# Sigmoid attention and a mixer in one kernel: which unit does which share of the channel products

## The chip, the cores and the metric

The kernel runs on one core of one Trainium2 chip. The metric is the device time of one execution in microseconds; the time before is 366.64 us, the median of three runs (366.64 to 368.11).

## The reference

Eight batches of twelve attention heads, 448 positions of 64 features, with a sigmoid in place of a softmax. The result, as 448 x 768 per batch, goes through a mixer: a token product over the positions (448 to 256 to 448) with a residual, then a channel product over the features (768 to 1536 to 768) with a residual.

```python
scores = scale * np.matmul(q, k.transpose(0, 1, 3, 2)) - np.log(S)
attn = 1.0 / (1.0 + np.exp(-scores))
x = np.matmul(attn, v)                        # as (8, 448, 768)
xt = x.transpose(0, 2, 1)
h = np.maximum(xt @ w_tok1, 0.0) @ w_tok2     # token product
u = x + h.transpose(0, 2, 1)
h2 = np.maximum(u @ w_ch1, 0.0) @ w_ch2       # channel product
out = u + h2
```

## The kernel before

The instructions stand in the order in which the code issues them (`tc.manual_schedule()`); each engine works through its own list in order and waits on semaphores that the tile framework places. All products take 16-bit floats and accumulate in PSUM.

**Units.** The twelve heads of a batch are worked on four at a time, so a batch has NU = 3 units u = 0, 1, 2, and there are 24 of them; unit c is batch c // 3, u = c % 3. In unit c TensorE does:

- `qk`, seven score steps (j = 0 to 6). Each is four products on 64x64 quarters of the array (L174) into one of two score tiles; ScalarE then makes one sigmoid of it (L181).
- `av` for unit c - 1: the value product, 28 quarter products (L201) into two PSUM banks, cast by VectorE to xT (L210). `xtrans_dma` (L225), on SP's queue, transposes xT into xn.
- the token product of unit c - 2: `tok_tail` (L260, quarter tiles) and `tok1` (L279, full tiles), two relus on ScalarE (L293), then `ytrans` (L300), the second token product, whose result VectorE adds to xT, giving u (L307).
- a share of the channel products of an earlier batch: `ch1` (twelve tiles of 128 channels, six products each, L333; relu on VectorE, L345) and `ch2` (for three blocks t of 128 positions two halves of 384 features, twelve products each, L402; the addition of u on VectorE, L426), and `ch2_last`, the half block of 64 positions that remains (24 products of 128x64, two side by side, L486; L511). Batch 0's u has no transposed copy `un`, so there TensorE adds it, by products with the identity (L414, L497).

**Quarter products of the channel part.** `ch1_pair` and `ch2_pair` do a part of two such tiles with the 64x64 quarters of the array (`quads`, L357), four at once, so that the array keeps the shape that the scores and the value product have. `turn0` and `turn1` are the two passes over the rows of the array; `ch2_pair` does eight of the twelve terms so and leaves four for each half to `rest` (L462), on full tiles.

**PSUM.** The two score tiles take four of the eight banks; the other four, m0 to m3, are handed out by `bank`, in turn from `at_bank`. A tile that gets a bank waits for the reader of the tile that had it. `keep_open` skips a bank in which a tile is being accumulated.

**Stages.** An opening written out by hand does units 0 to 3 and the first two tiles of batch 0's ch1. A first loop (L728 on, `range(N_FIRST, ONE_RUN)`) does units 4 to 8, with the channel work cut into pieces (`pieces_ch1`, `pieces_ch2`, `pieces_last`) and set between groups of score steps by shares: batch 0's remaining ch1 and its ch2 over units 4 to 7, batch 1's ch1 in unit 8. A second loop does units 9 to 23, where all work on quarter tiles is in one run: score steps 0 and 1, `turn0`, step 2, `av` with step 3, step 4, `turn1` with step 5, `tok_tail`, step 6. Behind the run come, on full tiles, `rest`, `tok1`, pieces of channel work and `ytrans`. Of batch b - 2, u = 0 does the c2 pair of t = 0 and the half block, u = 1 the c2 pair of t = 1 and both halves of t = 2 in full tiles; of batch b - 1, u = 2 does a c1 pair and the other ten tiles of ch1. A closing does the last value and token products, batch 6's ch2 and batch 7's channel products.

**Loads.** q, k, v and the weights come by POOL's queue (`load`). From batch 2 on q and k are put into another order by VectorE (`relayout`, L119, three for each) and transposed by a DMA on SP's queue (`dma_transpose`, L132), in the list `through_dma`, of which the loops take one item at a time (`copies.pop(0)()`). `gated_loads(b)` on POOL waits, by a small copy (L714), for the transposed q of batch b + 1, and then issues the loads of v for batch b + 1 and of k and q for batch b + 2. `utrans` transposes u into `un` on SP's queue.

Of the kernel before, what the change touches and what calls it, by code (L numbers as in the profile page):

```python
# [22 lines left out]
NU = 3  # L23


@with_exitstack
def kernel(
# [46 lines left out]
    at_bank, open_bank = [0], [None]  # L74
# [9 lines left out]
    def keep_open(is_open):  # L84
        open_bank[0] = (at_bank[0] + 3) % 4 if is_open else None
# [239 lines left out]
    def ch1(b, cb, d0=0, d1=NDB):  # L325
        if cb == 0 and d0 == 0:
            h2[b] = pa.tile([128, NCB, S], FP16, tag="h2", bufs=1, name=f"h2_{b}")
        if d0 == 0:
            acc[b, cb] = bank([128, 512], FP32, f"c1_{b}_{cb}")
            keep_open(b != 0 or cb > 1)  # L330
        ps = acc[b, cb]
        for d in range(d0, d1):
            nc.tensor.matmul(  # L333
                out=ps[:, 0:S],
                lhsT=c1[:, BY_UNIT[d], 128 * cb : 128 * cb + 128],
                rhs=uts[b % 2][:, BY_UNIT[d], 0:S],
                start=(d == 0),
                stop=(d == NDB - 1),
            )
        if d1 == NDB:  # L340
            keep_open(False)
            ch1_out(b, cb, ps)
# [22 lines left out]
    def ch1_pair(b, cb):  # L365

        if cb == 0:
            h2[b] = pa.tile([128, NCB, S], FP16, tag="h2", bufs=1, name=f"h2_{b}")
        ps = [bank([128, 512], FP32, f"c1_{b}_{cb + p}") for p in range(2)]

        def step(turn, d):
            quads(
                ps,
                S,
                turn,
                lambda p, part, m: c1[
                    part, BY_UNIT[d], 128 * (cb + p) + m : 128 * (cb + p) + m + 64
                ],
                lambda p, part: uts[b % 2][part, BY_UNIT[d], 0:S],
                d == 0,  # L380
                d == NDB - 1,
            )
            if turn == 1 and d == NDB - 1:
                for p in range(2):
                    ch1_out(b, cb + p, ps[p])

        turns = [[lambda t=t, d=d: step(t, d) for d in range(NDB)] for t in range(2)]
        return turns[0], turns[1], lambda: None

# [3 lines left out]
    def ch2(b, t, half, n0=0, n1=NCB):  # L393
        cols = slice(DH * half, DH * half + DH)
        if n0 == 0:
# [3 lines left out]
            keep_open(True)  # L399
# [11 lines left out]
        keep_open(False)  # L411
        if b not in un:
            for n in range(NU):
                nc.tensor.matmul(  # L414
                    out=ps[:, 128 * n : 128 * n + 128],
                    lhsT=uts[b % 2][:, NU * half + n, 128 * t : 128 * t + 128],
                    rhs=ident[:, :],
                    start=False,
                    stop=(n == NU - 1),
                )  # L420
        ch2_out(b, t, half, ps)

# [18 lines left out]
    def ch2_pair(b, t):  # L441
# [17 lines left out]
        def rest():  # L459
            for p in range(2):  # L460
                for n in range(n_quads, NCB):
# [5 lines left out]
                        stop=(n == NCB - 1),  # L467
                    )
                ch2_out(b, t, p, ps[p])
# [256 lines left out]
    ONE_RUN = 3 * NU  # L726
    pending, copies = [], []
    for c in range(N_FIRST, ONE_RUN):  # L728
        b, u = divmod(c, NU)
        before = divmod(c - 1, NU)  # L730


        if c in (N_FIRST, 2 * NU + 2):
# [26 lines left out]
        if c == 2 * NU + 2:  # L760
            copies += through_dma(3, 0)[NU + 1 :]
# [14 lines left out]
        if c == 2 * NU + 1:  # L776
            copies = through_dma(3, 0)[: NU + 1]
        spent += work(2)
        if c == 2 * NU + 2:
            utrans(b - 1)  # L780
# [8 lines left out]
        if c + 1 == ONE_RUN:  # L789
            at_bank[0] = 0  # L790
# [9 lines left out]
    for c in range(ONE_RUN, N_CYCLES):  # L800
# [20 lines left out]
        qk(b, u, 2)  # L821
        if u == 2:
            utrans(b - 1)
        av(*before, 0, 4)
# [9 lines left out]
        at_bank[0] = 0  # L834
# [11 lines left out]
        at_bank[0] = 0  # L846
# [23 lines left out]
    for f in work[20:]:  # L870
# [33 lines left out]
```

## Time and profile before

| | |
|---|---|
| runs | 366.64, 368.11, 366.64 us |
| profiled execution | 366.46 us, of which the profile's span is 364.7 |
| granted TensorE clock | 0.999 |
| TensorE's products by line, busy us | ch1 L333 100.6; qk L174 60.3; ch2 L402 58.1; av L201 41.0; quarter products L357 32.0 (c2) and 14.9 (c1) |
| sigmoids L181 | 168 of 1015 ns, 155.6 us busy |

A row of the timeline has the start in us, the length, engine, line, operation, output <- inputs, their sizes and the count of instructions merged into it; in square brackets stands the idle time of the engine just before, with what ended it. Products overlap: the next one starts before the one before has ended, so what a product costs is read from start to start and not from its length. A row of the stages has the stretch, its length, and for each engine the busy time and the count of instructions, then the clock, the DMA engines' share and GB/s. "PEld" is TensorE's loading of weights.

### The profile page before, as it was taken

The page shows a single profiled execution, that of the slowest core. Times are in us where ns is not written, and L with a number is a line of the kernel's source. Part 1 is how long each engine was busy: PE and PEld are TensorE (multiplying, and loading weights), DVE is VectorE, ACT ScalarE, POOL GpSimd, SP SyncE. Part 2 cuts the span into 40 slices and gives each one's busy share as a digit, 9 for nine tenths or more (in the row PEclk, how much of TensorE's full clock was granted, in tenths as well). Part 3 has the DMA queues.
Part 4 walks back from the last instruction along what each step waited for, and adds up shares of the span by engine and source line. Part 5 has one row for each costly group of instructions (what it writes and reads, how often), then busy time and mean ns, then how long its engine had stood idle before and what let it go on. Part 6 is the DMA issues. An engine that isn't in the chain of part 4 may idle for free.

```text
span 364.7 us, 8938 instructions
## 1 busy us (share of the span) xinstructions
PE 354.8 (97%) x3968; PEld 207.2 (57%) x3968; DVE 186.2 (51%) x343; ACT 171.3 (47%) x214; POOL 52.8 (14%) x91
## 2 busy tenths in 40 slices
PE   8889999999999999999999999999999999999995
PEld 5555455556556665665655665566656665555563
DVE  3466547355645456455554565455553445525531
ACT  2996545767246770664516761664607751010000
POOL 8875500120120002200040001300010000000000
PEclk9999999999999999999999999999999999999999
DMA  8999999999999398977989497987983274137014
GB/s 146 163 192 203 204 204 193 141 182 213 181 174 162 80 165 157 191 132 154 182 132 215 70 190 149 176 149 147 174 134 81 59 155 43 31 86 130 23 45 108
DMA packets 103958, 52.09 MB, mean 143 GB/s; under 512 B 76016, under 2 KB 100848, under 8 KB 103920
## 3 DMA queue, kind: packets, MB, share of 16 engines
q1 hardware_dynamic: 78880, 29.70, 43.8%
q0 software_dynamic: 24816, 21.50, 38.2%
q8 instruction: 31, 0.51, 0.5%
q10 hardware_dynamic: 224, 0.33, 0.3%
q14 instruction: 7, 0.06, 0.1%
HBM read 43.45 MB, written 11.01 MB: 149 GB/s over the span
## 4 chain that ended last, share of the span: by engine, by line
PE 89%; DMA 4%; POOL 4%; ACT 1%; DVE 0%; issue 0%; POOLq 0%
PE c L333 27%; PE c L402 15%; PE c L357 11%; PE qk L174 9%; PE xa L201 8%; PE yt L300 5%; PE tk L279 5%; PE c L486 5%; PE c L462 4%; DMA raw_q<-in_q_dram 2%; DMA raw_v<-in_v_dram 2%; POOL raw_q L108 1%; POOL raw_k L108 1%; POOL raw_v L108 1%; ACT att L181 1%
## 5 line engine op out<-in xcount | busy, mean ns | idle before, releaser
L181 ACT ACTIVATE att<-qk,att_bias 128x896 f16<-128x896 f32 x168 | 155.6, 1015 | 119.7 <-PE qk L174 119.0
L333 PE MATMUL c<-ut,c 128*128 128x448 f16 x516 | 100.6, 353 | 0.7 <-DVE h L345 0.7
L345 DVE TENSOR_SCALAR h<-c 128x448 f16<-128x448 f32 x96 | 59.2, 623 | 46.9 <-PE c L333 46.0
L333 PEld LDWEIGHTS <-c 128*128 128x128 f16 x516 | 49.6, 98 | 48.4 <-issue 4.4
L174 PE MATMUL qk<-tr_q,tr_k 64*64 64x448 f16 x672 | 60.3, 357 | 2.1 <-ACT att L181 2.0
L402 PE MATMUL c<-c,h 128*128 128x384 f16 x336 | 58.1, 326 | 0.0
L210 DVE CAST xT<-xa 128x448 f16<-128x448 f32 x48 | 27.7, 619 | 40.2 <-PE xa L201 40.2
L426 DVE TENSOR_TENSOR o<-un,c 128x384 f32<-128x384 f16 x42 | 23.3, 554 | 46.1 <-PE c L402 31.0
L402 PEld LDWEIGHTS <-h 128*128 128x128 f16 x336 | 32.1, 98 | 21.7 <-issue 1.8
L201 PE MATMUL xa<-att,raw_v 64*64 64x448 f16 x672 | 41.0, 350 | 0.0
L174 PEld LDWEIGHTS <-tr_k 64*64 64x64 f16 x672 | 22.8, 105 | 21.4 <-issue 15.6
L357 PE MATMUL c<-c,h 64*64 64x384 f16 x640 | 32.0, 323 | 0.0
L307 DVE TENSOR_TENSOR ut<-xT,yt 128x448 f16<-128x448 f16 x48 | 27.5, 614 | 4.4 <-PE yt L300 4.1
L714 POOL COPY gate<-tr_q 128x2 f16<-128x2 f16 x6 | 1.1, 184 | 194.1 <-DMA tr_q<-rel_q 194.1
L201 PEld LDWEIGHTS <-raw_v 64*64 64x64 f16 x672 | 22.4, 107 | 10.7 <-issue 2.2
L293 ACT ACTIVATE h<-tk 128x256 f16<-128x256 f32 x42 | 14.5, 395 | 29.6 <-PE tk L279 29.6
L357 PEld LDWEIGHTS <-h 64*64 64x64 f16 x640 | 19.9, 107 | 8.2 <-DVE o L511 1.5
L300 PE MATMUL yt<-w,h 128*128 128x448 f16 x96 | 22.2, 353 | 0.3 <-DVE h L345 0.3
L279 PE MATMUL tk<-xn,w 128*128 128x256 f16 (+1 forms) x156 | 21.7, 274 | 0.0
L279 PEld LDWEIGHTS <-w 128*128 128x128 f16 (+1 forms) x156 | 14.2, 98 | 6.4 <-issue 3.1
L486 PE MATMUL c<-c,h 128*64 128x384 f16 x192 | 17.3, 328 | 0.0
L108 POOL DMA_DIRECT2D raw_q<-in_q_dram x26 | 16.7, 658 | 3.4 <-DMA w2s<-in_moe_w_tok_dram 1.2
(55 smaller groups left out, 199.5 us busy)
## 6 DMA issues: line engine op xcount, KB each, us to landing
out_dram<-o SPq DMA_DIRECT2D x48, 192.0 KB, 3.0
c<-in_moe_w_ch_dram POOLq DMA_DIRECT2D x4, 1152.0 KB, 15.2
raw_v<-in_v_dram POOLq DMA_DIRECT2D x12, 336.0 KB, 5.6
raw_k<-in_k_dram POOLq DMA_DIRECT2D x10, 336.0 KB, 8.0
raw_q<-in_q_dram POOLq DMA_DIRECT2D x10, 336.0 KB, 10.3
raw_q<-in_q_dram POOLq DMA_DIRECT2D x14, 112.0 KB, 6.1
out_dram<-o SPq DMA_DIRECT2D x15, 96.0 KB, 2.5
raw_k<-in_k_dram POOLq DMA_DIRECT2D x12, 112.0 KB, 5.8
```

The costliest lines, as they stand in the source:

```text
L108: nc.gpsimd.dma_start(out=dst.rearrange("p u hi j e -> p (u hi) (j e)"), in_=heads.rearrange("h (p j) e -> p h (j e)", j=NJ),)
L174: nc.tensor.matmul(out=ps[64 * g : 64 * g + 64, hi, 0:S], lhsT=tr[b, "k"][64 * hi : 64 * hi + 64, u, j, 64 * g : 64 * g + 64], rhs=tr[b, " ...
L181: nc.scalar.activation(out=att[b, u][:, :, j, :], in_=ps[:, :, 0:S], func=SIGMOID, bias=bias_t[:, :], scale=att_scale,)
L201: nc.tensor.matmul(out=ps[g][64 * hi : 64 * hi + 64, 0:S], lhsT=raw[b, "v"][64 * g : 64 * g + 64, u, hi, j, :], rhs=att[b, u][64 * g : 64 ...
L210: nc.vector.tensor_copy(out=xTs[b % 2][:, u, g, 0:S], in_=ps[g][:, 0:S])
L279: nc.tensor.matmul(out=ps[tcb], lhsT=w1[rows, t, cols], rhs=xn[b][rows, u, :, t, :], start=(t == 0 and not with_scores), stop=(t == (2 if ...
L300: nc.tensor.matmul(out=ps[:, 0:S], lhsT=h1[b][:, tcb, g, u, :], rhs=w2[:, tcb, :, :], start=(tcb == 0), stop=(tcb == 1),)
L333: nc.tensor.matmul(out=ps[:, 0:S], lhsT=c1[:, BY_UNIT[d], 128 * cb : 128 * cb + 128], rhs=uts[b % 2][:, BY_UNIT[d], 0:S], start=(d == 0), ...
L345: nc.vector.tensor_scalar(out=h2[b][:, cb, :], in0=ps[:, 0:S], scalar1=0.0, scalar2=None, op0=MAX)
L357: nc.tensor.matmul(out=ps[p][m : m + 64, 0:n], lhsT=lhsT(p, part, m), rhs=rhs(p, part), start=(first and turn == 0), stop=(last and turn = ...
L402: nc.tensor.matmul(out=ps[:, 0:DH], lhsT=h2[b][:, cb, 128 * t : 128 * t + 128], rhs=c2[:, cb, cols], start=(cb == 0), stop=(cb == NCB - 1 ...
L486: nc.tensor.matmul(out=ps[g], lhsT=h2[b][:, n, 384:448], rhs=c2[:, n, DH * g : DH * g + DH], start=(n == 0), stop=(n == NCB - 1 and not ad ...
```

## The change

- `ONE_RUN` goes from 3·NU to 2·NU: the second loop now begins at unit 6 and not at unit 9.
- In the second loop every unit does a c2 pair of batch b - 2, for t = u. In u = 2 the half block of batch b - 2 and all twelve tiles of ch1 of batch b - 1 follow on full tiles; in u = 0 and 1 nothing follows but `ytrans`. There is no c1 pair any more.
- The first loop does only batch 0's ch1, with shares of 21 and 9 for units 4 and 5; batch 0's ch2 is done by the c2 pairs of units 6 to 8, which add u by products with the identity (`add_u`).
- Behind the run `tok1` comes first and then `rest`.
- The re-layouts and DMA transposes of batch b + 1 are taken up two at a time in u = 1 (behind score step 2 and behind `rest`) and in u = 2 (behind score step 2), then by the pieces of ch1; batch 3's are set up in unit 7, the others' in u = 0.
- Banks: in the opening (up to unit 5) they come from a list, `OPENING_BANKS`, one digit for each tile in the order of the code; `keep_open` is gone. In the second loop the pair takes m2 and m3, the value product, the token product and ytrans m0 and m1, the half block m1, and ch1 all four from m0.
- In the closing four pieces of batch 6's ch2 come ahead of the last value product, and the later cuts move by four.

```diff
+OPENING_BANKS = "032130213021302121302130302130212130213013021032103210"
...
     def bank(shape, dtype, name):
-        if at_bank[0] == open_bank[0]:
-            at_bank[0] = (at_bank[0] + 1) % 4
-        tag = f"m{at_bank[0]}"
-        at_bank[0] = (at_bank[0] + 1) % 4
-        return pp.tile(shape, dtype, tag=tag, bufs=1, name=name)
+        if opening_banks:
+            n = opening_banks.pop(0)
+        else:
+            n = at_bank[0]
+            at_bank[0] = (n + 1) % 4
+        return pp.tile(shape, dtype, tag=f"m{n}", bufs=1, name=name)
...
+    def add_u(b, t, half, ps):
+        for n in range(NU):
+            nc.tensor.matmul(
+                out=ps[:, 128 * n : 128 * n + 128],
+                lhsT=uts[b % 2][:, NU * half + n, 128 * t : 128 * t + 128],
+                rhs=ident[:, :],
+                start=False,
+                stop=(n == NU - 1),
+            )
...
-                        stop=(n == NCB - 1),
+                        stop=(n == NCB - 1 and b in un),
                     )
+                if b not in un:
+                    add_u(b, t, p, ps[p])
                 ch2_out(b, t, p, ps[p])
...
-    ONE_RUN = 3 * NU
+    ONE_RUN = 2 * NU
+    LATER = 3
...
-            if c == N_FIRST:
-                pending, shares = stage2(0, by_half=True)[4:], [9, 9, 6, 6]
-            else:
-                pending, shares = list(pieces_ch1(1)), [30]
+            pending, shares = list(pieces_ch1(0))[4:], [21, 9]
...
-        lot = b - 1 if u == 2 else b - 2
-        at_bank[0] = 2
-        if u == 2:
-            turn0, turn1, rest = ch1_pair(lot, 0)
-            work = pieces_ch1(lot, 2)
-        elif u == 0:
-            turn0, turn1, rest = ch2_pair(lot, 0)
-            work = pieces_last(lot)
-        else:
-            turn0, turn1, rest = ch2_pair(lot, 1)
-            work = pieces_ch2(lot, [(2, 0), (2, 1)])
+        X, Y = 2, 0
+        at_bank[0] = X
+        turn0, turn1, rest = ch2_pair(b - 2, u)
...
         qk(b, u, 2)
+        if copies:
+            copies.pop(0)()
+            copies.pop(0)()
         if u == 2:
             utrans(b - 1)
+        at_bank[0] = Y
...
         qk(b, u, 6)
+        tok1(*ahead, with_scores=True)
         rest()
-        tok1(*ahead, with_scores=True)
-        at_bank[0] = 2
-        if u == 0 and b + 1 < B:
+        if u == 1 and copies:
+            copies.pop(0)()
+            copies.pop(0)()
+        if u == 0 and LATER < b + 1 < B or u == 1 and b + 1 == LATER:
             copies = through_dma(b + 1, 0)
-        for n, (w, f) in enumerate(work):
-            f()
-            if copies and n % 2 == 1:
-                copies.pop(0)()
-        at_bank[0] = 0
+        if u == 2:
+            at_bank[0] = Y + 1
+            for w, f in pieces_last(b - 2):
+                f()
+            at_bank[0] = Y
+            for n, (w, f) in enumerate(pieces_ch1(b - 1)):
+                f()
+                if copies and n % 2 == 1:
+                    copies.pop(0)()
+        at_bank[0] = Y
         ytrans(*ahead)
...
+    at_bank[0] = X
+    for f in work[:4]:
+        f()
     av(*before)
     xtrans_dma(*before)
-    for f in work[:12]:
+    for f in work[4:12]:
         f()
     tok1(*ahead)
-    for f in work[12:16]:
+    for f in work[12:20]:
         f()
     tok1(*before)
-    for f in work[16:20]:
+    for f in work[20:24]:
         f()
     ytrans(*ahead)
     ytrans(*before)
     utrans(B - 1)
-    for f in work[20:]:
+    for f in work[24:]:
         f()
```

More of the change, by code (lines that the diff above doesn't have):

```diff
@@ L72 @@
     uts = [pc.tile([128, NDB, 512], FP16, name=f"ut{n}") for n in range(2)]
-    at_bank, open_bank = [0], [None]
+    opening_banks = [int(n) for n in OPENING_BANKS]
+    at_bank = [0]
     def bank(shape, dtype, name):
-        if at_bank[0] == open_bank[0]:
-            at_bank[0] = (at_bank[0] + 1) % 4
-        tag = f"m{at_bank[0]}"
-        at_bank[0] = (at_bank[0] + 1) % 4
-        return pp.tile(shape, dtype, tag=tag, bufs=1, name=name)
-    def keep_open(is_open):
-        open_bank[0] = (at_bank[0] + 3) % 4 if is_open else None
+        if opening_banks:
[4 more added lines that the diff above has]
+        return pp.tile(shape, dtype, tag=f"m{n}", bufs=1, name=name)
     raw, rel, tr = {}, {}, {}
@@ L340, in ch1 @@
         if d1 == NDB:
-            keep_open(False)
             ch1_out(b, cb, ps)
@@ L363, in quads @@
                 )
[L365 to L388, printed above, removed]
     outs = {}
@@ L398, in ch2 @@
             acc[b] = bank([128, 512], FP32, f"c2_{b}_{t}_{half}")
-            keep_open(True)
         ps = acc[b]
@@ L410, in ch2 @@
             return
-        keep_open(False)
         if b not in un:
[L413 to L420, printed above, removed]
-        ch2_out(b, t, half, ps)
+            add_u(b, t, half, ps)
+        ch2_out(b, t, half, ps)
+    def add_u(b, t, half, ps):
[7 more added lines that the diff above has]
+            )
     def ch2_out(b, t, half, ps):
@@ L730 @@
         before = divmod(c - 1, NU)
-        if c in (N_FIRST, 2 * NU + 2):
+        if c == N_FIRST:
             first = c
-            if c == N_FIRST:
-                pending, shares = stage2(0, by_half=True)[4:], [9, 9, 6, 6]
-            else:
-                pending, shares = list(pieces_ch1(1)), [30]
+            pending, shares = list(pieces_ch1(0))[4:], [21, 9]
             total = sum(w for w, f in pending)
```

11 lines of the change are left out of this document (1 added, 10 removed).

## The prediction

> **What bounds the kernel now.** I call one (batch, u) step of the attention loop a unit and number it 3·batch + u: seven score steps, the value product of the unit before, the token product of the unit before that, and a share of channel work. The page comes first.
>
> ```profile
> span 364.7 us, 8938 instructions
> PE 354.8 (97%) x3968; PEld 207.2 (57%) x3968; DVE 186.2 (51%) x343; ACT 171.3 (47%) x214; POOL 52.8 (14%) x91
> ```
>
> TensorE is busy for 97% of the span; VectorE and ScalarE have half their time free. The profiled execution took 366.46 us, 1.76 us more than its span, and the median is 0.18 us above it. As the change leaves the sum of products as it is, only what TensorE loses between products can move the time: changes of tile shape, waits inside a unit, waits of the opening. So I cut the busy times into stages at the first score step of each unit. First units 5 to 8, then batch 4 (units 12 to 14, which later batches repeat) and unit 22; columns are the stretch, its length, then PE, PEld, DVE, ACT and POOL.
>
> ```profile
> 55.25:67.14 11.89, 11.89 (x135) 6.48 (x134) 7.98 (x15) 6.61 (x7) 0.00 (x0) 1.00 1.34 179
> 67.14:77.21 10.07, 10.07 (x110) 5.50 (x108) 3.30 (x7) 7.16 (x9) 2.82 (x5) 1.00 0.78 136
> 77.21:87.70 10.49, 10.49 (x125) 5.99 (x124) 5.64 (x12) 7.16 (x9) 0.00 (x0) 1.00 1.10 222
> 87.70:106.75 19.05, 18.71 (x145) 9.67 (x144) 12.22 (x22) 7.16 (x9) 4.15 (x7) 1.00 1.02 178
> ...
> 148.15:158.62 10.47, 10.47 (x167) 6.51 (x166) 4.73 (x10) 7.11 (x9) 0.00 (x0) 1.00 1.27 198
> 158.62:171.22 12.60, 12.60 (x167) 7.95 (x166) 6.88 (x14) 7.21 (x9) 0.00 (x0) 1.00 0.54 125
> 171.22:189.55 18.33, 18.30 (x180) 10.57 (x179) 10.78 (x20) 6.94 (x9) 4.13 (x7) 1.00 0.91 154
> ...
> 282.83:295.09 12.26, 12.26 (x168) 7.54 (x168) 5.19 (x11) 7.10 (x9) 0.00 (x0) 1.00 0.33 71
> ```
>
> A batch takes 10.47 + 12.60 + 18.33 = 41.40 us. ScalarE is busy 7.1 us in every unit, so a unit can't fall much below 8 us. The clock is full (1.00) in each. The order of TensorE's work inside units 12 and 14, from the timeline (start, length):
>
> ```profile
> 148.15 0.57 PE L174 MATMUL qk<-tr_q,tr_k 64*64 64x448 f16 x8
> 148.55 1.47 PE L357 MATMUL c<-c,h 64*64 64x384 f16 x32
> 149.85 0.36 PE L174 MATMUL qk<-tr_q,tr_k 64*64 64x448 f16 x4
> ...
> 153.34 0.36 PE L174 MATMUL qk<-tr_q,tr_k 64*64 64x448 f16 x4
> 153.63 1.47 PE L462 MATMUL c<-c,h 128*128 128x384 f16 x8
> 154.94 0.82 PE L279 MATMUL tk<-xn,w 128*128 128x256 f16 x6
> 155.69 2.14 PE L486 MATMUL c<-c,h 128*64 128x384 f16 x24
> 157.76 0.93 PE L300 MATMUL yt<-w,h 128*128 128x448 f16 x4
> ...
> 176.68 0.83 PE L279 MATMUL tk<-xn,w 128*128 128x256 f16 x6
> 177.35 11.51 PE L333 MATMUL c<-ut,c 128*128 128x448 f16 x60
> 188.70 0.92 PE L300 MATMUL yt<-w,h 128*128 128x448 f16 x4
> ```
>
> From start to start: the run of 64x64 tiles with a c2 pair, 153.63 - 148.15 = 5.48; the pair's last eight products, 1.31; the token product, 0.75 with a change of tile shape behind it, 0.67 without (177.35 - 176.68); the last half block (L486), 2.07; ytrans up to the next unit, 158.62 - 157.76 = 0.86; sixty ch1 products, 11.35, so 72 take 13.62.
>
> **The steady batches (3 to 7).** Units u = 0 and 1 lose their full-tile channel work (L486, or two c2 groups), and u = 2 takes the third c2 pair for the c1 pair, then L486, then all 72 ch1 products. The counts over a batch don't change, nor does the price of a pair: the row at 148.55 shows 32 quarter products in 1.30, against eight full ones in 1.31. In u = 0 and 1 nothing but the pair's rest stands between the token product and ytrans, which needs the token product's two relus on ScalarE. What hides them there is in unit 14, where the token product already follows the last score step at once:
>
> ```profile
> 177.96 0.70 ACT L293 ACTIVATE h<-tk 128x256 f16<-128x256 f32 x2
> ```
> The relus end at 178.66, 7.44 after the unit's start at 171.22. TensorE would reach ytrans at 5.48 + 0.67 + 1.31 = 7.46, and only its second product needs the second relu; for the wake-up I add 0.05 (bounds: 0 and 0.3, one relu's share of that 0.70). So u = 0 and 1 take 7.46 + 0.05 + 0.86 = 8.37 each. If the cover went, because the relus came as late as in unit 13's run, the price is that of the slow rival below. In u = 2 the last half block reuses the bank of the second relu, the same wait: 5.48 + 0.67 + 1.31 + 0.08 (tile shape, 0.75 - 0.67) + 0.05 + 2.07 + 13.62 + 0.86 = 24.14. A batch is then 40.88, or 0.52 less than 41.40.
>
> Part of that 0.52 is a disturbance that these rows show in unit 13, against 12.26 in unit 22, which has no re-layout:
>
> ```profile
> 151.76 1.15 DVE L210 CAST xT<-xa 128x448 f16<-128x448 f32 x2 [2.58 <-PE xa L201]
> ...
> 154.49 1.20 DVE L426 TENSOR_TENSOR o<-un,c 128x384 f32<-128x384 f16 x2 [1.35 <-PE c L462]
> ...
> 159.04 0.62 DVE L119 COPY rel_k<-raw_k 128x896 f16<-128x896 f16 x1
> 159.69 1.15 DVE L307 TENSOR_TENSOR ut<-xT,yt 128x448 f16<-128x448 f16 x2
> ...
> 159.06 1.12 PEld L357 LDWEIGHTS <-h 64*64 64x64 f16 x32 [0.30 <-DVE o L511]
> ```
>
> In unit 13 the pair's weights wait for an eviction (L511), then a re-layout stands ahead of ytrans's additions, which hold the banks of the value product: 12.60 - 12.26 = 0.34. After the change the pair's two evictions, which end 155.69 - 153.63 = 2.06 after its rest begins, end 6.15 + 2.06 = 8.21 after the unit's start, and the next pair begins at 8.37 + 0.40: 0.56 to spare. Two re-layouts (2 x 0.62) stand behind the third score step of u = 1 and of u = 2, in VectorE's queue from about 1.8 to 3.0 after the unit's start; the casts there come 151.76 - 148.15 = 3.6 after the unit's start. So they are hidden with 0.6 to spare. Behind a late re-layout the casts queue, and for these wait the token product's banks and the transpose on SP's queue; a late raw load would cost its whole delay. Batch 7 has no re-layouts to lose: its gain is 0.52 - 0.34 = 0.18. The steady sum is 4 x 0.52 + 0.18 = 2.3 us less. Its bounds: relus 0.3 late in each of the 15 units, 3.75 lost, so 1.5 slower; no wait at all, 3.0 faster.
>
> **Units 5 to 8.** Batch 0's c2 product leaves units 5 to 7 for the pairs of units 6 to 8. Unit 5 loses 24 full products (3 x 1.31 = 3.93) and two identity groups; the row of one is
>
> ```profile
> 64.76 0.33 PE L414 MATMUL c<-ident,ut 128*128 128x128 f16 x3
> ```
>
> half of which overlaps its neighbour: 0.35 for both (bounds 0.16 and 0.66). That leaves 11.89 - 4.28 = 7.61. Units 6 and 7 are steady u = 0 and 1 plus the identity groups, 8.37 + 0.35 = 8.72; unit 6 pays 0.3 more by estimate, since unit 5's seven sigmoids (6.61 busy) start some 0.5 after its products and end after them, and unit 6's second score step needs the last one's bank. Unit 8 is 24.14 + 0.45 = 24.59 (half a group more for the last half block). Sum 49.94 against 11.89 + 10.07 + 10.49 + 19.05 = 51.50: 1.6 less. Most of it is fewer changes between quarter and full tiles: three score groups amid full products become one run. Bounds: 0 and 2.2.
>
> **Transfers that this pulls forward.** Loads don't move with TensorE there, so I check each against its new user.
>
> ```profile
> L565 POOL DMA_DIRECT2D c<-in_moe_w_ch_dram x2: 1033/1042/1052, 34.3 to 43.0; - x2
> DMA to landing us min/median/max: 15.8/16.6/17.3
> ...
> raw_k<-in_k_dram POOLq DMA_DIRECT2D x10, 336.0 KB, 8.0
> ...
> tr_q<-rel_q SPq DMA_TRANSPOSE x6, 5.1
> ```
>
> The second half of c2 lands by 43.0 + 17.3 = 60.3; unit 6 needs it, new, at about 61.8 + 0.4. The transposed q of batch 2 is issued some 1.7 after unit 5's end, behind two re-layouts, and needed 7 us later, against 5.1. Batch 3's leaves SP after 12 ch1 pieces of unit 8, 7.7 us before unit 9; the gate on POOL opens 5.1 later, and raw k, some 2 us on in POOL's queue and 8.0 to land (10 for its second half), comes 1 to 3 us before its re-layout in unit 10. All hidden, by 1 us at the least.
>
> **The bank list.** Units 0 to 3 keep their order, unit 4 takes one ch1 piece earlier; the banks change. Three waits of TensorE there are bank waits:
>
> ```profile
> 24.05 1.16 DVE L210 CAST xT<-xa 128x448 f16<-128x448 f32 x2 [0.29 <-PE xa L201]
> 24.73 0.58 PE L154 MATMUL tp_q<-ident,raw_q 128*64 128x128 f16 x14 [0.53 <-DVE xT L210]
> ...
> 31.15 1.15 DVE L210 CAST xT<-xa 128x448 f16<-128x448 f32 x2
> 31.82 0.58 PE L154 MATMUL tp_q<-ident,raw_q 128*64 128x128 f16 x14 [0.71 <-DMA raw_q<-in_q_dram]
> 32.65 0.62 PE L234 MATMUL xb<-ident,xT 128*128 128x128 f16 x8
> ...
> 48.38 1.86 PE L333 MATMUL c<-ut,c 128*128 128x448 f16 x9 [0.71 <-DVE h L345]
> ```
>
> Before, each of these tiles took the bank last used by a tile still being evicted (the second row names a DMA, but the start follows the first cast's end). By the list each takes a bank evicted earlier. The first gains nothing: the transposes of x next in line wait for the same casts. The second gains 0.4, until its own casts end at 32.30 instead of the 32.65 shown. The third gains its 0.71. Together 1.1; bounds 0 and 1.95.
>
> **The rest at nothing.** In the closing, four c2 pieces move ahead of the last value product: same products, same changes of shape. Four fewer full pieces stand between the last ytrans and batch 7's ch1. What hides its four additions (2 x 1.15 = 2.3) is ytrans and the last half block, 1.6 + 2.07; without these it would cost at most 2.3.
>
> **Sum.** 2.3 + 1.6 + 1.1 = 5.0: span 364.7 - 5.0 = 359.7, the execution 361.5, and with 0.18 for the median 361.6 us.
>
> A page's rule speaks against it. The row: 32 quarter products in 1.30, no dearer than full ones, and 107 ns for one load of their weights (the page's group):
>
> ```profile
> L357 PEld LDWEIGHTS <-h 64*64 64x64 f16 x640 | 19.9, 107 | 8.2 <-DVE o L511 1.5
> ```
>
> The Trainium skill, TensorEngine Tiling, Restrictions and Gotchas, says that column tiling excludes the fast weight load, so quarter tiles could be held up by their weights; by that rule the time could go to that of the last rival. The trace of before disagrees, with 880 such products at no extra price.
>
> **The rivals.**
> 1. Loads set the opening: the gain of units 2 to 8 is given back at a later load or transposed q, whose landing doesn't move. For it: DMA shares of 1.0 to 1.3 there. Against: the spare times above. 366.64 - 2.3 = 364.3 us.
> 2. The steady batches gain nothing, because ytrans in u = 0 and 1 and the last half block in u = 2 wait 0.17 more each. For it: only 0.02 lies between 7.44 and 7.46. Against: unit 14's relus end there to the row. 366.64 - 2.7 = 363.9 us.
> 3. Slower: every run is disturbed as in unit 13, since now every unit begins with a pair on banks that were evicted last. That cost 0.34 there; in 18 units it is 6.1: 361.6 + 6.1 = 367.7 us. It decides from 0.28 a unit (5.0 / 18). For it: the wait for L511 stands in all five batches (1.5 in the row above). Against: the 0.56 to spare, where before had none.
> 4. The change doesn't do what it says: the banks only move their waits (0), units 5 to 8 stay at their bound (0), and the relus come 0.2 late (15 x 0.15 = 2.3): 366.6 us. Against: three causes at once.
> 5. Weights bound the added quarter products: 1152 - 880 = 272 of them (18 pairs of 64, against 10 of 64 and 5 of 48), or 68 groups of four. Four loads one behind the other, 4 x 0.107 instead of 1.30 / 8 = 0.163, add 68 x 0.27 = 18: 380 us.
>
> **How the numbers follow.** Forecast 0.55, rivals 0.14, 0.12, 0.10, 0.08 and 0.01. The forecast's own range goes halfway to the upper and lower ends of the parts taken together (7.2 and -1.5 off 366.6): 360.5 to 364.9. To hold 8 in 10 the range takes in rivals 1 and 2 and stops short of 4 and 3, as the costs of new waits are the least known: up to 366.0; downward it goes nearly to all upper ends (359.5), with some for gains that I don't see: 358.8. About 0.5% (1.8 us) is what a measurement of this kernel can tell from no change: faster is below 364.8, so nearly all of the forecast and of rivals 1 and 2, 0.79; same 0.10; slower 0.11.
>
> **What would show it.** Right: units of about 8.4, 8.4 and 24.1 us per batch by the first score steps; unit 9 starting near 104 instead of 106.75; no idle time before the second tp_q (31.82 above) and the sixth c1 tile (48.38); relus ending 7.4 after the unit's start. Wrong: ytrans waiting for L293's relus, the pair's weights waiting for VectorE, re-layouts standing in VectorE's queue for a raw load, a score step waiting for transposed q, or a unit 9 that starts no earlier.

## The result, and the profile after

The kernel after the change takes 365.78 us, the median of 14 runs (363.29 to 366.70), against 366.66 for the kernel before in 14 runs beside it: 0.9 us less by the medians. The ratio of the means is 0.9961 (365.59 to 367.02), 95% interval 0.9942 to 0.9980. That is inside the 0.5% that counts as no change here, and not the 361.6 of the forecast. The ratios leave out slow executions: one of the kernel before here (920.7 us) and two of e4 below (369.83 and 370.31 us). The profiled execution took 365.41 us with a span of 363.6, where the forecast had 359.7.

First the page of the kernel after: the span, the engines, and the chain of work that ended last, by line.

```profile
span 363.6 us, 9352 instructions
PE 351.2 (97%) x4172; PEld 204.7 (56%) x4172; DVE 185.5 (51%) x343; ACT 168.9 (46%) x214; POOL 53.0 (15%) x91
...
PE c L333 30%; PE c L356 10%; DMA xn<-xT 9%; PE qk L175 8%; PE xa L202 7%; PE c L375 7%; PE c L437 6%; PE tk L280 5%; PE c L463 5%; PE yt L301 5%; ACT att L182 4%; DMA raw_q<-in_q_dram 1%; PE tk L261 1%; PE tp_k L155 1%; DVE xT L211 1%
```

TensorE's busy time fell by 3.6 us (354.8 to 351.2), the span only by 1.1. The chain says where to look: a DMA, xn<-xT, which is the transpose of the value product for the token product, now stands on it with 9% of the span. Next the stages of the kernel after, cut at the first score steps: units 5, 6, 8, 10, 13 and 14 (stretch, length, busy time and count of PE, PEld, DVE, ACT and POOL, clock, DMA share, GB/s).

```profile
53.15:61.26 8.11, 7.84 (x103) 3.81 (x103) 5.75 (x11) 6.31 (x7) 0.00 (x0) 1.00 1.30 203
61.26:71.67 10.41, 8.88 (x149) 6.23 (x148) 4.23 (x9) 7.25 (x10) 0.07 (x1) 1.00 1.30 171
...
80.31:106.05 25.74, 24.97 (x253) 14.03 (x252) 15.17 (x28) 7.06 (x9) 0.34 (x2) 1.00 0.95 162
...
114.34:124.66 10.32, 8.50 (x144) 5.18 (x143) 4.58 (x10) 7.06 (x9) 0.00 (x0) 1.00 1.17 170
...
157.22:165.52 8.30, 8.30 (x143) 5.33 (x142) 4.58 (x10) 6.95 (x9) 0.00 (x0) 1.00 0.45 98
165.52:189.78 24.26, 24.26 (x239) 13.48 (x238) 14.15 (x26) 6.95 (x9) 3.46 (x7) 1.00 0.81 152
```

Unit 14 takes 24.26, unit 13 8.30, and so do unit 9 and the other units u = 0 and 1 from unit 12 on. Units 6, 8 and 10 stand out: the stretch is longer than PE's busy time next to it by 1.5, 0.8 and 1.8 us. The view of waits of the kernel after names one reason for all three (engine, line, releaser: total us, times, longest):

```profile
PE tk L261 <- DMA xn<-xT: 4.1, 3, 1.8
```

The timeline of the kernel after shows what happens at the first of them, and, in its last row, the relus of unit 14:

```profile
56.50 1.32 SPq L226 DMA_TRANSPOSE xn<-xT  x1
60.42 5.59 SPq L133 DMA_TRANSPOSE tr_k<-rel_k  x1
66.06 3.38 SPq L133 DMA_TRANSPOSE tr_q<-rel_q  x1
...
65.88 0.69 PE L356 MATMUL c<-c,h 64*64 64x384 f16 x12
68.10 0.30 PE L261 MATMUL tk<-xn,w 64*64 64x256 f16 x4 [1.53 <-DMA xn<-xT]
...
172.26 0.70 ACT L294 ACTIVATE h<-tk 128x256 f16<-128x256 f32 x2
```

In unit 6 the pair's twelve last quarter products start at 65.88, and `tok_tail` (L261) can't start before 68.10, because the transpose of unit 4's value product, issued at 56.50, is still under way. In unit 14, which doesn't wait, `tok_tail` starts 0.48 after the same twelve products (170.12 and 170.60). By that measure TensorE loses 1.74 us in unit 6, and in the same way 0.95 in unit 8 (84.90 and 86.33) and 2.00 in unit 10 (118.94 and 121.42): 4.7 in all. Why the transpose is late is in the transfers of the kernel after, tile by tile: the row of an issue has its duration in ns and its first and last start, the row below how long until it landed.

```profile
L755 POOL DMA_DIRECT2D w<-in_moe_w_tok_dram x1: 533/533/533, 51.5 to 51.5; - x1
DMA to landing us min/median/max: 16.2/16.2/16.2
...
L226 SPq DMA_TRANSPOSE xn<-xT x1: 1317/1317/1317, 56.5 to 56.5; - x1
DMA to landing us min/median/max: 11.6/11.6/11.6
...
L109 POOL DMA_DIRECT2D raw_q<-in_q_dram x2: 675/681/687, 73.9 to 74.5; - x2
DMA to landing us min/median/max: 10.0/10.6/11.3
...
L226 SPq DMA_TRANSPOSE xn<-xT x1: 1782/1782/1782, 76.7 to 76.7; - x1
DMA to landing us min/median/max: 9.6/9.6/9.6
...
L109 POOL DMA_DIRECT2D raw_q<-in_q_dram x2: 669/672/675, 109.1 to 109.8; - x2
DMA to landing us min/median/max: 9.6/10.4/11.2
...
L226 SPq DMA_TRANSPOSE xn<-xT x1: 1260/1260/1260, 111.1 to 111.1; - x1
DMA to landing us min/median/max: 10.3/10.3/10.3
...
DMA to landing us min/median/max: 3.0/3.1/11.6
```

The last row is over all twenty transposes: the median is 3.1 us. The three late ones take 9.6 to 11.6, and each lands just after the last load that was issued before it (the first row is w1's last rows, the others raw q): 68.1 against 51.5 + 16.2 = 67.7; 76.7 + 9.6 = 86.3 against 74.5 + 11.3 = 85.8; 111.1 + 10.3 = 121.4 against 109.8 + 11.2 = 121.0.

Set against the forecast by stages (us; from the starts of units 5, 9 and 12 in each trace; the forecast's last two rows are 41.40 - 0.52 and 216.54 - 3 x 0.52 - 0.18):

| stretch | before | forecast | after |
|---|---|---|---|
| start of unit 5 | 55.25 | 54.15 | 53.15 |
| units 5 to 8 | 51.50 | 49.94 | 52.90 |
| units 9 to 11 | 41.40 | 40.88 | 42.87 |
| unit 12 to the span's end | 216.54 | 214.80 | 214.71 |

Up to unit 5 the change gains nearly twice what was forecast (1.0 more), and the last row meets the forecast within 0.1. Units 5 to 11 take 4.95 more than forecast, which makes the span 3.9 longer than the forecast's.

### The profile page after: what moved, and what is told of

It is laid out like the page before. It is cut to its first block, busy times and chain, and to the rows that moved or that the text cites. A ratio compares the mean times of both kernels' runs of the same rounds, so it can differ in the third digit from the quotient of the medians.

```text
span 363.6 us, 9352 instructions
## 1 busy us (share of the span) xinstructions
PE 351.2 (97%) x4172; PEld 204.7 (56%) x4172; DVE 185.5 (51%) x343; ACT 168.9 (46%) x214; POOL 53.0 (15%) x91
## 4 chain that ended last, share of the span: by engine, by line
PE 84%; DMA 10%; ACT 4%; DVE 1%; issue 1%; POOL 0%; POOLq 0%
PE c L333 30%; PE c L356 10%; DMA xn<-xT 9%; PE qk L175 8%; PE xa L202 7%; PE c L375 7%; PE c L437 6%; PE tk L280 5%; PE c L463 5%; PE yt L301 5%; ACT att L182 4%; DMA raw_q<-in_q_dram 1%; PE tk L261 1%; PE tp_k L155 1%; DVE xT L211 1%
## 5 line engine op out<-in xcount | busy, mean ns | idle before, releaser
L333 PE MATMUL c<-ut,c 128*128 128x448 f16 x576 | 112.7, 353 | 0.0
L333 PEld LDWEIGHTS <-c 128*128 128x128 f16 x576 | 54.6, 98 | 55.7 <-issue 4.4
L175 PE MATMUL qk<-tr_q,tr_k 64*64 64x448 f16 x672 | 57.8, 356 | 2.4 <-ACT att L182 2.3
L356 PE MATMUL c<-c,h 64*64 64x384 f16 x1152 | 56.1, 322 | 0.0
L356 PEld LDWEIGHTS <-h 64*64 64x64 f16 x1152 | 34.1, 107 | 13.8
L202 PE MATMUL xa<-att,raw_v 64*64 64x448 f16 x672 | 39.6, 349 | 0.0
L175 PEld LDWEIGHTS <-tr_k 64*64 64x64 f16 x672 | 21.3, 104 | 21.4 <-issue 14.2
L437 PE MATMUL c<-c,h 128*128 128x384 f16 x144 | 26.8, 326 | 0.0
L202 PEld LDWEIGHTS <-raw_v 64*64 64x64 f16 x672 | 20.1, 107 | 10.7 <-issue 0.3
L375 PE MATMUL c<-c,h 128*128 128x384 f16 x144 | 24.2, 326 | 0.0
L375 PEld LDWEIGHTS <-h 128*128 128x128 f16 x144 | 13.8, 98 | 9.6 <-issue 0.4
L437 PEld LDWEIGHTS <-h 128*128 128x128 f16 x144 | 14.0, 98 | 7.0
```

Of the source, the lines that this page charges most:

```text
L175: nc.tensor.matmul(out=ps[64 * g : 64 * g + 64, hi, 0:S], lhsT=tr[b, "k"][64 * hi : 64 * hi + 64, u, j, 64 * g : 64 * g + 64], rhs=tr[b, " ...
L202: nc.tensor.matmul(out=ps[g][64 * hi : 64 * hi + 64, 0:S], lhsT=raw[b, "v"][64 * g : 64 * g + 64, u, hi, j, :], rhs=att[b, u][64 * g : 64 ...
L333: nc.tensor.matmul(out=ps[:, 0:S], lhsT=c1[:, BY_UNIT[d], 128 * cb : 128 * cb + 128], rhs=uts[b % 2][:, BY_UNIT[d], 0:S], start=(d == 0), ...
L356: nc.tensor.matmul(out=ps[p][m : m + 64, 0:n], lhsT=lhsT(p, part, m), rhs=rhs(p, part), start=(first and turn == 0), stop=(last and turn = ...
L375: nc.tensor.matmul(out=ps[:, 0:DH], lhsT=h2[b][:, cb, 128 * t : 128 * t + 128], rhs=c2[:, cb, cols], start=(cb == 0), stop=(cb == NCB - 1 ...
L437: nc.tensor.matmul(out=ps[p][:, 0:DH], lhsT=h2[b][:, n, 128 * t : 128 * t + 128], rhs=c2[:, n, DH * p : DH * p + DH], start=False, stop=(n ...
```

## The experiments

The theory after this reading: the change's products gain what was forecast, and the waits of `tok_tail` for late transposes take it away. The rivals: the regrouping of units 5 to 8 is dear by itself; and the list's gain in the opening can't be kept, whatever waits, because loads set the pace there. Each experiment was timed in five to twelve executions beside the kernel before, whose median was 366.59 for e1 to e4 and 366.84 for e5 to e7. Their profiles, by the same stretches as above (span at the end):

| | to unit 5 | units 5 to 8 | units 9 to 11 | to the end | span |
|---|---|---|---|---|---|
| e1, waits taken away | 53.78 | 51.53 | 41.31 | 214.7 | 361.3 |
| e2, list only | 54.69 | 50.99 | 41.40 | 216.6 | 363.6 |
| e3, second loop only | 55.41 | 51.49 | 40.86 | 214.7 | 362.5 |
| e4, loads in another order | 53.33 | 55.31 | 40.86 | 214.7 | 364.2 |
| e5, list and second loop | 53.15 | 51.00 | 40.86 | 214.7 | 359.7 |
| e6, batch 3's transposes earlier | 54.85 | 50.30 | 40.86 | 214.7 | 360.7 |
| e7, change without the list | 56.96 | 50.21 | 43.08 | 214.7 | 365.0 |

The first column has to be read with care. A profile is one execution, and some have a late start: in the stage of unit 1 of e6 the clock was 0.87 for the stretch (0.84 and 0.86 in e2 and e7), and the unit took 7.57 us instead of 6.68.

```profile
14.40:21.97 7.57, 6.07 (x72) 3.32 (x72) 3.25 (x5) 7.13 (x8) 4.97 (x8) 0.87 1.20 179
```

**e1: the late transposes taken away.** In the kernel after, the token products of units 6, 8 and 10 read an xn that landed long before, and the load of w1's last 64 rows, which competes with the first, is left out. So these three token products compute something else.

```diff
+    def landed(b, u):
+        return {4: (1, 0), 6: (1, 2), 8: (2, 0)}.get(NU * b + u, (b, u))
...
-                    rhs=xn[b][part, u, :, 3, :],
+                    rhs=xn[landed(b, u)[0]][part, landed(b, u)[1], :, 3, :],
...
-        if c == N_FIRST:
-            nc.gpsimd.dma_start(out=w1[64:128, 3, :], in_=tok_rows[NJ - 1])
```

> The changed kernel, but the token products of units 6, 8 and 10 read an xn that landed a unit or more earlier, and the late load of w1's last 64 rows is left out: the computation of those three token products is changed, the work is not. Theory (the missing time is TensorE waiting in units 6, 8 and 10 for xn's transpose, which lands behind the raw loads): the three waits of 1.8, 1.1 and 2.1 us go, the units take about 8.7, 8.6 + 16 and 8.3 us, span near 359, execution near 361. Rival (the start of those units is held by the loads anyway, so a wait removed here comes back at the transposed q or at the value product): span 362 to 364, with waits of the score steps or of the value product in units 7 to 12. The before kernel stays at 366.6.

Measured: 361.16 us (360.74 to 363.10), ratio 0.9844 (0.9815 to 0.9873). By the medians that is 4.6 us less than the kernel after, so nearly all of the 4.7 come back, and the time is close to the forecast's. The profiled execution was the slowest of the six (363.10), and its stretches from unit 5 to 11 gain 2.9. The stages of units 6, 8 and 10 in e1, and the row of its timeline that holds what is left:

```profile
61.89:71.90 10.01, 8.89 (x149) 7.20 (x149) 5.21 (x10) 7.18 (x10) 0.00 (x0) 1.00 1.33 163
...
80.54:105.31 24.77, 24.77 (x251) 14.18 (x251) 15.18 (x28) 6.95 (x9) 0.25 (x2) 1.00 0.92 163
...
113.61:122.36 8.75, 8.59 (x144) 5.33 (x143) 4.58 (x10) 7.06 (x9) 0.00 (x0) 1.00 1.40 189
```

```profile
71.90 0.57 PE L175 MATMUL qk<-tr_q,tr_k 64*64 64x448 f16 x8 [1.12 <-DMA tr_q<-rel_q]
```

Unit 8 is down from 25.74 to 24.77 and unit 10 from 10.32 to 8.75. Unit 6 gains only 0.4 in this execution: once `tok_tail` runs on time, the first score step of unit 7 waits 1.1 us for the transposed q of batch 2. That is one of the waits that the prediction held to be covered. The other executions have no profile, so how often this wait comes isn't known.

**e2: only the list of banks**, in the kernel before (its first 45 tiles; then in turn as before).

```diff
+        if opening_banks:
+            n = opening_banks.pop(0)
+            at_bank[0] = (n + 1) % 4
+            return pp.tile(shape, dtype, tag=f"m{n}", bufs=1, name=name)
```

> The kernel before with the list of banks up to unit 4's channel tiles, nothing else. Theory (bank waits; the trace of after shows unit 5 starting 2.1 us earlier): unit 5 starts at 53.2 instead of 55.25 and the end comes 1.5 to 2.1 us earlier, 364.5 to 365.1, as no token product of before is close to its transpose. Rival (loads hold units 5 to 9): the gain is lost by unit 9, execution 366 to 366.6.

Measured: 364.13 us (363.94 to 365.40), ratio 0.9919 (0.9894 to 0.9944): 2.5 us less. By itself the list is worth more than twice the forecast's 1.1.

**e3: only the second loop's new order**, in the kernel before, from unit 9 on (no list, units 5 to 8 as before).

```diff
+        turn0, turn1, rest = ch2_pair(b - 2, u)
...
+        tok1(*ahead, with_scores=True)
         rest()
-        tok1(*ahead, with_scores=True)
...
+        if u == 2:
+            at_bank[0] = Y + 1
+            for w, f in pieces_last(b - 2):
+                f()
+            at_bank[0] = Y
+            for n, (w, f) in enumerate(pieces_ch1(b - 1)):
```

> The kernel before with the new second loop from unit 9 on; opening, first loop and closing as before. Theory: batches of 40.9 instead of 41.4 us, 2.3 us less in all, execution 364.3, perhaps with one wait for xn in unit 10 of up to 1 us (365.3). Rival (the steady batches owe their gain to the earlier start): no gain, 366.6.

Measured: 364.27 us (364.13 to 366.19), ratio 0.9926 (0.9899 to 0.9953): 2.3 us less, which is the forecast's term for the steady batches. Unit 10 doesn't wait here: units 9 to 11 take 40.86, as short as in any run.

**e4: the loads in another order.** In the kernel after, the load of batch 2's v is held back until unit 4's transpose has landed, and batch 3's re-layouts and transposes are issued at every piece of ch1 in unit 8 instead of every other.

```diff
-    load(2, "v", v, 0, NU)
...
+        if c == N_FIRST + 1:
+            nc.gpsimd.tensor_copy(out=gate[:, :], in_=xn[1][:, 1, 1, 3, 126:128])
+            load(2, "v", v, 0, NU)
...
-                if copies and n % 2 == 1:
+                if copies and (n % 2 == 1 or b + 1 == LATER):
                     copies.pop(0)()
```

> The changed kernel with batch 2's v loaded only when xn of unit 4 has landed, and batch 3's re-layouts and transposes taken up with every ch1 piece of unit 8 instead of every second, so that the loads of the next batch begin 3 us earlier. Theory (xn's transpose lands when the raw loads ahead of it have landed): xn of unit 4 lands before 65 and unit 6's wait goes; unit 8's shrinks; unit 10's shrinks from 2.1 to under 0.5; span 359.5 to 361, execution 361.3 to 362.8. Rival (transposes are slow by themselves there, or wait for their issue): waits of the same length, execution 365 to 366; or a new wait of unit 7's value product for v, up to 3 us.

Measured: 365.52 us, the median of ten executions (363.48 to 367.34), ratio 0.9953 (0.9928 to 0.9979), so no clear gain over the kernel after. The transfers of e4: unit 4's transpose, now 6.5 us instead of 11.6, and the transposed q of batch 2, 10.3 instead of 5.4; then the row of the timeline where the wait went.

```profile
L226 SPq DMA_TRANSPOSE xn<-xT x1: 1316/1316/1316, 56.7 to 56.7; - x1
DMA to landing us min/median/max: 6.5/6.5/6.5
...
L133 SPq DMA_TRANSPOSE tr_q<-rel_q x1: 2233/2233/2233, 63.3 to 63.3; - x1
DMA to landing us min/median/max: 10.3/10.3/10.3
```

```profile
73.55 0.87 PE L175 MATMUL qk<-tr_q,tr_k 64*64 64x448 f16 x8 [3.24 <-DMA tr_q<-rel_q]
```

The waits of units 6, 8 and 10 are gone. In unit 6 that is what should come if loads made the transpose late. In unit 10 it goes with the gate on POOL, which opens 4.2 us before unit 9 (104.49 and 108.64) and not 0.7 as in the kernel after. Unit 8 shows nothing: its transpose lands at 80.3 + 7.0 = 87.3, no earlier than the 86.3 of the kernel after, and is in time because unit 7 started and ended later. The load that was moved now runs beside the next transpose, and TensorE stands still for 3.2 us before unit 7. Another order of v alone moves the wait and doesn't end it; the DMA share of 1.3 in this stretch of the kernel after (1.27 here) fits with transfers that can only take time from each other, but no run tests that by itself.

**e5: list and second loop**, in the kernel before: e2 and e3 together, that is, the whole change but for the regrouping of units 5 to 8 and the new order of the closing.

> The kernel before with the list of banks up to unit 4 and the new second loop from unit 9 on, so the change without its regrouping of units 5 to 8. Theory (the list and the loop keep what they gain, and the regrouping is what brings transposes and loads too close): the gains add, 2.5 + 2.3 off 366.6, execution 361.5 to 362.3, faster than the changed kernel by about 4 us; no wait for xn above 0.3 us. Rival (an opening that is faster by 2 us is itself too early for the loads of the new loop): waits in units 9 and 10, execution 363 to 365.

Measured: 361.64 us (361.50 to 363.02), ratio 0.9841 (0.9817 to 0.9866). This is faster than both kernels. The gains of e2 and e3 add up (2.5 + 2.3 = 4.8; measured 5.2 by the medians). Unit 4's transpose is as slow here (11.7), but `tok_tail` of unit 6, in the old order of units 5 and 6, first needs it at 69.0; it landed at 56.5 + 11.7 = 68.2. From the tiles of e5, its first start and the landings of all twenty:

```profile
L267 PE MATMUL tk<-xn,w x72: 269/269/269, 69.0 to 289.3; 64*64 64x256 f16 x72
...
DMA to landing us min/median/max: 3.0/3.3/11.7
```

**e6: batch 3's transposes earlier.** The kernel after with only the last hunk of e4.

> The changed kernel with batch 3's re-layouts and transposes taken up with every ch1 piece of unit 8, and nothing else. Theory (unit 10 waits because batch 4's loads, released by the transposed q of batch 3, are still under way): the release comes 3 us earlier, unit 10's wait of 2 us shrinks to 0 to 0.5, those of units 6 and 8 stay at about 1.8 and 1.1; execution 363.5 to 364.5. Rival (unit 10's wait has another cause): unit 10 stays above 10 us, execution 365.8.

Measured: 362.64 us (362.50 to 363.58), ratio 0.9871 (0.9845 to 0.9897). The stages of units 6, 8 and 10 of e6, then its transpose for unit 10:

```profile
62.96:71.65 8.69, 8.69 (x150) 6.38 (x150) 4.24 (x9) 7.13 (x10) 0.19 (x2) 1.00 1.17 175
...
80.28:105.15 24.87, 24.87 (x253) 14.04 (x252) 15.04 (x28) 6.94 (x9) 3.19 (x6) 1.00 1.03 174
...
113.45:121.75 8.30, 8.30 (x145) 5.32 (x144) 4.58 (x10) 6.94 (x9) 0.00 (x0) 1.00 0.81 126
```

```profile
L226 SPq DMA_TRANSPOSE xn<-xT x1: 1232/1232/1232, 110.2 to 110.2; - x1
DMA to landing us min/median/max: 6.7/6.7/6.7
```

By the medians this gains 3.1 us over the kernel after, more than unit 10's wait and more than expected. The gate on POOL opens at 101.04 instead of 105.38, the loads behind it are that much further on, and the transpose takes 6.7 us instead of 10.3. That accounts for the 2.0 of unit 10. Units 6 and 8 have their `tok_tail` ahead of that gate; that they don't wait in this profile (0.1 us in unit 8) goes with its late start, by which they came later against the loads, so one execution doesn't settle how the medians' 3.1 us divide.

**e7: the change without the list.** The kernel after with the old way of handing out banks in the opening.

```diff
+        if opening_left[0] and at_bank[0] == open_bank[0]:
+            at_bank[0] = (at_bank[0] + 1) % 4
...
+    def keep_open(is_open):
+        open_bank[0] = (at_bank[0] + 3) % 4 if is_open else None
```

> The changed kernel with the old way of handing out banks in the opening in place of the list. Theory (from unit 6 on transfers set the pace, so what the list gains is waited away): unit 5 starts 2.1 us later, unit 6's wait for xn falls by about as much, unit 7 starts within 0.5 us of the changed kernel's 71.7, and the end is within 0.7 us of the changed kernel's 365.8. Rival (the list's gain is kept): about 368.

Measured: 366.13 us (364.86 to 367.92), ratio 0.9964 (0.9943 to 0.9984). The stages of units 6 and 10:

```profile
65.07:73.76 8.69, 8.69 (x150) 6.38 (x150) 4.24 (x9) 7.13 (x10) 1.13 (x3) 1.00 0.95 155
...
115.47:125.98 10.51, 8.49 (x143) 5.17 (x143) 4.67 (x10) 7.05 (x9) 0.00 (x0) 1.00 1.19 169
```

So the list is worth 2.5 us in the kernel before (e2) and 0.35 in the kernel after (366.13 - 365.78). The units that start later without it don't wait: 8.69 instead of 10.41 in unit 6. Unit 10 waits as before, because its loads hang on the gate behind unit 8 and move with it. Unit 7 starts at 73.76, so the expectation of 0.5 us around 71.7 was missed: 1.1 of the 2.1 is this execution's late start (unit 2 starts at 22.02 instead of 20.96), and the other 1.0 comes back in unit 8. So the stages alone don't prove the point. The medians of e2 and e7 carry it, and the 0.35 is smaller than the scatter of either kernel.

## Why the prediction was wrong

**The steady batches: right.** Units of 8.30, 8.30 and 24.26 against 8.37, 8.37 and 24.14, a batch of 40.86 against 40.88. That the sum is met so closely is partly luck: no relu was waited for, which gives 0.07 in each of the two short units, and the 72 ch1 products of unit 14 take 13.80 (175.14 to 188.94), 0.18 more than the 13.62 that were scaled up from sixty. The relus of unit 14 end at 172.26 + 0.70 = 172.96, which is 7.44 after the unit's start, as in the kernel before. e3 has the whole term, 2.3 us, by itself. Rival 2 (relus that come late), rival 3 (pairs that wait for evictions; it would need 0.28 a unit) and rival 5 (weights) show nothing in these units.

**The list: too small.** It brings unit 5 forward by 2.10, from 55.25 to 53.15, against 1.1. That is above its upper bound of 1.95. By units, 0.53 comes in unit 2, 0.51 in unit 3 and 1.08 in unit 4. The mis-sized parts are the first wait, put at nothing because the transposes of x were thought to wait for the same casts (in the kernel after, the fourteen products of tp_q run while the casts do), and the third, put at the 0.71 of its row alone, though the products around it were held up too. e2 gives 2.5 by the medians, with unit 8 half a microsecond shorter as well (18.54 instead of 19.05), where ytrans had waited for a relu's bank.

**Units 5 to 8: the products right, the waits missed.** Without waits they take 8.11 + 8.69 + 8.63 + 24.77 = 50.20 (e7's profile has them so, 50.21), against 49.94; 0.5 of unit 5 is score steps that wait for sigmoids, which the prediction had put at 0.3 and in unit 6. The kernel after took 52.90. And the comparison was too kind: with the list in place the old order takes 51.00 (e5), so that regrouping had 0.8 us to give at most, not 1.6.

**Transfers: the step that failed.** "All hidden, by 1 us at the least" was said of c2, the transposed q and raw k. The transposes of xn were not in that list, so their wait was put at nothing. xn of unit c - 2 is issued in unit c - 1 and used in unit c, and both became shorter: in the kernel after 9.9, 8.7 and 8.4 us lie between its issue and the moment when units 6, 8 and 10 would use it, where the kernel before had 12.5, 14.2 and 10.8. And the transposes became slower: 11.6, 9.6 and 10.3 us, where the same three took 6.7, 4.4 and 3.9 in the kernel before. That cost 4.7 us, or more than the whole difference. The prediction checked transfers that got a new user, and none whose old user comes earlier or that would run beside other loads than before.

In unit 10 the shorter units alone are not the cause, since e3 has the same two units of 8.30 us there and no wait. There the gate on POOL that releases batch 4's loads opens at 98.91. In the kernel after the last transposes of batch 3 stand further back, among the pieces of unit 8, and the gate opens 6.9 us later than in the kernel before. So the loads were under way until 121.0, beside nearly all of xn's transpose (111.1 to 121.4), where in the kernel before the last one landed at 102.9 + 11.5 = 114.4. The gates of the kernel before and of the kernel after, then the transpose for unit 10 in the kernel before:

```profile
98.52 0.19 POOL L714 COPY gate<-tr_q 128x2 f16<-128x2 f16 x1 [23.71 <-DMA tr_q<-rel_q]
...
105.38 0.19 POOL L691 COPY gate<-tr_q 128x2 f16<-128x2 f16 x1 [30.19 <-DMA tr_q<-rel_q]
...
L225 SPq DMA_TRANSPOSE xn<-xT x1: 1232/1232/1232, 111.8 to 111.8; - x1
DMA to landing us min/median/max: 3.9/3.9/3.9
```

The prediction had the gate's shift (it put the gate 2.6 us before unit 9, and it came 0.7 before), but it asked only whether raw k would come in time. Raw k didn't: it landed at 107.8 + 9.2 = 117.0, and VectorE's re-layout in unit 10 waited 1.7 us for it, where 1 to 3 to spare had been forecast. In the kernel after that is hidden behind the wait for xn; in e1 it stays, and unit 10 takes 8.75 instead of 8.30.

The price of the transposed q was off as well: it left SP's queue at 66.06, 4.8 after unit 5's end instead of 1.7, because SP was held for 5.59 us by the issue ahead of it; it landed at 66.06 + 5.4 = 71.5, and the score step that needs it started at 71.67.

Of the rivals the first, that loads set the opening, was right in kind: the gain of units 2 to 8 was given back down to 0.7 (unit 9 starts at 106.05 instead of 106.75). Its price was too low, since unit 10 in the steady part lost 2.0 more. It had been judged by the spare times of other transfers. The fourth rival's time, 366.6, is near the measured one, but its causes are not: e2 and e3 have the gains that it took to be nothing. And that 365.78 lies just inside the stated range, which went up to 366.0, is no success of the mechanism; the range had been stretched for waits of unknown size.

**The closing: right.** From unit 12 to the end 214.71 against 214.80, and e3 and e5, which keep the old closing, have 214.7 too.

What stays open: in unit 6 the load of w1's last rows lands at 67.7, 0.4 before xn, and `tok_tail` needs both. Which alone would suffice wasn't tried. Nor was an order of all loads that keeps the regrouping free of waits. Whether it would save anything over e5 is not shown: e1 has the ratio 0.9844 and e5 0.9841.

## What to carry to other kernels

A unit that becomes shorter brings forward every user in it, also of transfers that the change doesn't touch; each of those transfers needs its own check. Its time in the old profile is not enough for that: the slowest landing of these transposes was 6.7 us there, which would have passed. What would have caught it is the question which loads will be under way beside it after the change, and when the last of them lands. Where the DMA engines have little to spare, as in the stretches here with shares of 1.0 to 1.3, a gain in the work beside them can be given back at the next landing, and gains that were measured apart needn't add: here two of three parts together (361.6) beat all three (365.8). So the parts are worth measuring apart, and in pairs.

## What the runs showed of the hardware

**A transpose by DMA beside bulk loads.** It took 3.1 us where no load was under way (issued at 69.49 in the kernel after) and 9.6 to 11.6 beside loads. Over the stretch from 53 to 70 us in the kernel after, the two queues had (packets, MB, share of 16 engines):

```profile
q0 software_dynamic: 2623, 2.06, 76.9%
q1 hardware_dynamic: 3638, 0.92, 52.6%
```

A packet of the loads (q0) thus took 0.769 x 16 x 17 / 2623 = 0.080 us, one of the transposes (q1) 0.526 x 16 x 17 / 3638 = 0.039, half as much. The Trainium skill, DMA: Bandwidth & Descriptors, Queues, rings and completion order, says that each DMA engine takes turns between its queues, a packet at a time. By that rule a transpose beside a load gets one third of the time, and 3 x 3.1 = 9.3 us is the estimate. The trace agrees roughly, with 9.6 to 11.6 here and 11.7 in e5. (The two shares add up to 1.3, so packets overlap in part and the estimate is a rough one.) The same transpose of unit 4 is quicker where the load beside it ends sooner: w1's load landed 5.7, 7.3 and 5.7 us after the transpose's issue in the kernel before, e6 and e7. With a third of the time up to there and all of it afterwards the estimates are 6.9, 8.0 and 6.9 us; measured were 6.7, 7.9 and 6.6.

**The clock after a stall.** The stages of e4 from the end of unit 6 on; the granted clock is the third column from the right.

```profile
69.70:73.55 3.85, 0.62 (x4) 0.20 (x2) 1.51 (x3) 0.00 (x0) 0.00 (x0) 1.00 1.40 192
73.55:75.00 1.45, 1.45 (x20) 1.09 (x23) 0.00 (x0) 0.85 (x1) 0.59 (x2) 0.55 1.23 285
75.00:76.50 1.50, 1.50 (x27) 1.14 (x23) 0.00 (x0) 1.06 (x2) 1.50 (x3) 0.50 0.78 159
76.50:78.00 1.50, 1.50 (x32) 1.12 (x28) 0.00 (x0) 0.66 (x1) 0.72 (x2) 0.80 0.86 103
78.00:79.50 1.50, 1.50 (x44) 1.21 (x37) 0.66 (x2) 1.50 (x3) 0.00 (x0) 1.00 1.23 195
```

After the 3.24 us without products the clock fell to half. By the shares of the three slow rows it stayed there for 1.3 + 1.5 + 0.6 = 3.4 us, and unit 7 took 10.32 us instead of 8.63: the stall cost half as much again behind it. The waits of 1 to 2 us in the kernel after left the clock at 1.00. The Trainium skill, TensorE: Matmul & The Clock Gate, Part 1: The HAM clock gate, gives an idle window of about 3.4 us after which the clock is halved, and about as long a busy one until it is full again. The trace agrees with the second within its resolution, and nearly with the first, as 3.24 us were enough here.

**Spread.** Kernels in which TensorE waits for such transposes scattered more from run to run: 363.3 to 366.7 after (14 executions), 363.5 to 367.3 in e4 (10), 364.9 to 367.9 in e7 (12), against 361.5 to 363.0 in e5 (5) and 366.4 to 368.5 in the kernel before (13 beside the kernel after). In what the fastest of them differ was not seen, since only one execution of each was profiled.
